# One exponential over two PSUM banks in the head of a fused attention and mixer kernel

## The chip, the cores and the metric

The kernel runs on one core of a Trainium2 chip. The metric is the device time of one execution in microseconds, the median of several; lower is better. The core's engines work side by side, each through its own queue in order: TensorE (PE), VectorE (DVE), ScalarE (ACT), GpSimd (POOL) and SyncE (SP), the last used for DMA alone. PSUM, where the matmuls write, is used as eight banks of 128 x 512 fp32 values.

## The reference

Two layers in a row, on 8 batches. The first is attention by random features (8 heads, 576 positions, 64 channels, 128 features), the second a mixer over tokens and channels.

```python
def phi(x):                                        # 128 features
    h = einsum('bhsd,md->bhsm', x, omega) - sum(x * x) / 2
    return exp(h - max(h)) / sqrt(m)
q_p, k_p = phi(q * scale), phi(k * scale)
kv  = einsum('bhsm,bhsd->bhmd', k_p, v);  z = sum(k_p, axis=2)
num = einsum('bhsm,bhmd->bhsd', q_p, kv)
den = einsum('bhsm,bhm->bhs', q_p, z)[..., None] + 1e-06
x = (num / den).transpose(0, 2, 1, 3).reshape(8, 576, 512)
h = maximum(x.transpose(0, 2, 1) @ w_tok1, 0) @ w_tok2     # 576 -> 256 -> 576
u = x + h.transpose(0, 2, 1)
out = u + maximum(u @ w_ch1, 0) @ w_ch2                    # 512 -> 1536 -> 512
```

## The kernel before, in words

All work is cut into some 1,200 jobs, each for one engine: a group of matmuls, an exponential, a copy, a DMA. `ORDER` is a list, written out in full, of the order in which the jobs are issued; a negative number there is a warming matmul on that bank, which computes nothing. `SLOT` gives, in the order in which they are asked for, the number of the buffer or PSUM bank that each job's result takes, and `MOVED` the jobs that run on another engine than usual. No scheduler decides anything later; each engine runs its jobs in the listed order, and semaphores keep the data in order between them. The eight banks are eight PSUM tiles, `bank0` to `bank7`.

A batch's 576 positions are 512 main positions and a tail of 64. For each batch the jobs are these:

- k and q come in. Batch 0's k is transposed on PE in fp32 (L470) and copied to `kT` (L286); q of batch 0 and k and q of batch 1 are transposed row by row in fp16 (`row_transposes`, L487) and copied to `qT` and `kT`. For k of batch 1, each of these copies has a small second one of the tails to `ktt` (four of 128 x 64). From batch 2 on, a DMA delivers them transposed.
- `attention`: for each of the four pairs of heads `hp`, `kp` (L642) and `qp` (L654) write the projected features of a pair into two banks, one for each half of the rows. Two exponentials for each, `kp_exp` and `qp_exp` (L516, 128 x 512, one for each bank), write `kp` and `qp` to SBUF. `km` (L666, L668) takes maxima of `kp` and their reciprocals on DVE; `vs` (L295) multiplies v by them, on POOL or DVE; `kv` (L687, with the tails L696) sums the products of `kp` and `vs`, and `kv_out` copies the result to `kvsb`. `num` (L720, L722) multiplies it with `qp` for one head, and `num_out` (L729, L730) divides on DVE; for two heads of batch 0 the division is a reciprocal on DVE (L739) and five scalings on ACT (L742).
- the tails: `kt` (L548), for batch 0 `kt_max` (L554) on DVE and four exponentials with that bias (L560); `qt` (L615) and `qt_exp`, two exponentials of 128 x 512 that read 256 columns each and write every value twice, to `qpt`.
- `token_mix_first` for batch 0: for each of four column blocks `db`, `t1` (L802, L803), a relu, `ut_` (L814, L816: x and the token product, summed in PSUM) and `ut_out`, the copy to `uT`. Later batches use `token_mix` and a transposing DMA.
- `channel_mix`: for each of 12 blocks `cb`, `c1` (L952) multiplies `uT` with a block of `wc1`, a relu follows, and `c2` (L986, for later batches L902) multiplies with `wc2`. For batch 0 and `cb` 0 and 1 the first product is split: `c1a` (L958) needs the first three blocks of `uT`, `c1b` (L960) the last.

The early part of the order mixes the attention of batches 0 and 1 with the loads of the weights; from the first `c1a` on, the products of one batch run beside the attention of the next.

Of the kernel before, what the change touches and what calls it, by code (L numbers as in the profile page):

```python
# [9 lines left out]
FP32 = mybir.dt.float32  # L10
# [71 lines left out]
]  # L82
SLOT = (
    "0001230450670021132045367010302617513012470262300513371400512200115470016321571004365170133427114615"
    "2706023150120733240065120734316732200715627122056371124763701250041207605411110007222613057312036204"
    "1375021106076210361724051016236170411507140350200761210416512307114506412733522052064330171260032070"
# [82 lines left out]
def kernel(  # L169
# [12 lines left out]
    nc = tc.nc  # L182
# [6 lines left out]
    P = 128  # L189
# [106 lines left out]

    def bank(name):
        return banks[place("bank", name)]

    def bank16(name):  # L300
        return bank(name).bitcast(FP16)

# [754 lines left out]
```

## Time and profile before

| | before |
|---|---|
| median of 3 runs | 278.24 us (277.53 to 278.56) |
| the profiled execution | 278.63 us, its span 276.8 us |
| PE busy | 269.2 us, 97% of the span, 2509 matmuls |
| DVE busy | 219.2 us, 79% |
| ACT busy | 141.1 us, 51% |
| POOL busy | 90.2 us, 33% |
| granted PE clock | 0.999 |

The span runs from the first to the last instruction that the profiler has; 1.83 us of the execution lie outside it. In the rows of the profile, names of buffers stand without their numbers, so that all of `bank0` to `bank7` are "bank". A row of a timeline gives the start and the duration in microseconds, the engine, the line, the operation with output and input, how many instructions the row holds, and in brackets the idle time of the engine before it with what ended it. A row of the chain of waits gives start, duration, engine, output and line of a piece of the chain that ended last.

### The profile page before, as it was taken

To read this page: it belongs to the slowest core of one execution; us is meant where nothing else is said; L and a number is where in the kernel's file an instruction comes from. 1 tells how busy PE (TensorE), PEld (TensorE's weight loads), DVE (VectorE), ACT (ScalarE), POOL (GpSimd) and SP (SyncE) were. 2 spreads that over 40 slices of the span, in tenths; PEclk is the share of its full clock that TensorE was granted. 3 is DMA by queue.
4 is the path that set the end of the run, shared out by engine and by line. 5 is a ranking of instruction groups with operands and counts; after the bars stand their busy time and mean duration, and the time that the engine had idled before them with its cause. 6 is when DMAs were issued, how large, how long until landed. Compare 5 with 4: busy or idle time off the path is not lost.

```text
span 276.8 us, 6243 instructions
## 1 busy us (share of the span) xinstructions
PE 269.2 (97%) x2509; PEld 167.5 (61%) x2509; DVE 219.2 (79%) x458; ACT 141.1 (51%) x296; POOL 90.2 (33%) x114
## 2 busy tenths in 40 slices
PE   7999999999999999999999999999999999999993
PEld 4467446455567655765676657755676477456782
DVE  2996948489996999996999899968985992685892
ACT  3999973288595237835756446635754500031200
POOL 8985482045812480076019510600043000000001
PEclk9999999999999999999999999999999999999999
DMA  7999999999999999869999994750252304030125
GB/s 194 193 204 204 198 201 183 203 160 147 206 207 142 221 182 163 206 120 167 176 202 175 252 109 129 170 113 2 85 90 77 96 0 94 2 152 0 78 82 147
DMA packets 81292, 39.66 MB, mean 143 GB/s; under 512 B 63984, under 2 KB 77040, under 8 KB 81072
## 3 DMA queue, kind: packets, MB, share of 16 engines
q0 software_dynamic: 31744, 17.74, 44.0%
q1 hardware_dynamic: 47360, 16.03, 28.3%
q10 hardware_dynamic: 2160, 5.51, 5.1%
q8 instruction: 19, 0.31, 0.4%
q14 instruction: 9, 0.07, 0.1%
HBM read 35.95 MB, written 16.52 MB: 189 GB/s over the span
## 4 chain that ended last, share of the span: by engine, by line
PE 87%; ACT 7%; DVE 3%; DMA 1%; issue 1%; ACTq 0%
PE bank L952 32%; PE bank L902 27%; PE bank L763 5%; PE bank L776 5%; PE bank L642 3%; PE bank L654 3%; PE bank L986 2%; PE bank L687 2%; PE bank L720 2%; ACT qp L516 2%; DMA wc<-in_k_dram 1%; DVE x L730 1%; PE bank L470 1%; ACT kp L516 1%; PE bank L830 1%; ACT r L290 1%
## 5 line engine op out<-in xcount | busy, mean ns | idle before, releaser
L290 ACT ACTIVATE r<-bank 128x512 f16<-128x512 f32 (+1 forms) x89 | 48.9, 599 | 82.5 <-PE bank L952 67.8
L952 PE MATMUL bank<-uT,wc 128*128 128x512 f16 x376 | 89.9, 379 | 0.0
L295 POOL TENSOR_TENSOR vs<-v,vs 128x512 f16<-128x512 f16 x31 | 32.7, 1060 | 91.8 <-DVE vs L668 62.5
L952 PEld LDWEIGHTS <-wc 128*128 128x128 f16 x424 | 38.6, 98 | 36.7 <-issue 0.3
L902 PEld LDWEIGHTS <-r 128*128 128x128 f16 x384 | 36.8, 98 | 8.8 <-issue 1.4
L516 ACT ACTIVATE qp<-bank 128x512 f16<-128x512 f32 x64 | 36.7, 633 | 9.3 <-PE bank L654 6.4
L516 ACT ACTIVATE kp<-bank 128x512 f16<-128x512 f32 x64 | 35.8, 626 | 7.3 <-PE bank L642 6.2
L666 DVE TENSOR_REDUCE km<-kp 128x8 f16<-128x1024 f16 x32 | 38.6, 1206 | 0.9 <-ACT kp L516 0.8
L730 DVE TENSOR_TENSOR x<-bank,rc 128x320 f16<-128x320 f32 x62 | 30.5, 491 | 2.1
L292 DVE TENSOR_SCALAR r<-bank 128x512 f16<-128x512 f32 (+1 forms) x37 | 24.6, 677 | 8.4 <-PE bank L952 7.5
L902 PEld LDWEIGHTS <-S 128*128 128x128 f16 x288 | 28.0, 98 | 5.1 <-issue 0.3
L902 PE MATMUL bank<-T,r 128*128 128x256 f16 x192 | 23.8, 273 | 0.0
L902 PE MATMUL bank<-wc,r 128*128 128x256 f16 x192 | 23.6, 273 | 0.0
L902 PE MATMUL bank<-T,S 128*128 128x256 f16 x192 | 23.4, 273 | 0.0
L891 DVE TENSOR_TENSOR o<-u,bank 128x512 f32<-128x512 f16 x28 | 19.0, 678 | 5.5 <-PE bank L902 5.4
L779 DVE TENSOR_TENSOR u<-x,bank 128x512 f16<-128x512 f16 x28 | 17.7, 680 | 4.9 <-PE bank L776 4.9
L931 POOL DMA_DIRECT2D out_dram<-o x2 | 1.3, 644 | 60.4 <-DVE o L891 60.4
L891 DVE TENSOR_TENSOR o<-o,bank 128x512 f32<-128x512 f32 (+1 forms) x27 | 16.5, 615 | 3.1 <-PE bank L902 2.6
L720 PEld LDWEIGHTS <-qp 128*128 128x128 f16 x256 | 13.7, 98 | 7.4 <-issue 0.3
L720 PE MATMUL bank<-kvsb,qp 128*128 128x65 f16 x256 | 15.4, 193 | 0.3 <-ACT kvsb L286 0.3
L729 DVE RECIPROCAL rc<-bank 128x5 f32<-128x5 f32 x62 | 11.4, 184 | 5.4 <-PE bank L722 4.2
L687 PEld LDWEIGHTS <-kp 128*128 128x128 f16 x256 | 11.2, 98 | 5.5 <-issue 0.9
(120 smaller groups left out, 381.6 us busy)
## 6 DMA issues: line engine op xcount, KB each, us to landing
out_dram<-o ACTq DMA_DIRECT2D x9, 512.0 KB, 2.7
q<-in_q_dram POOLq DMA_DIRECT2D x6, 576.0 KB, 9.9
wc<-in_moe_w_ch_dram POOLq DMA_DIRECT2D x4, 768.0 KB, 13.5
k<-in_k_dram POOLq DMA_DIRECT2D x6, 512.0 KB, 7.1
v<-in_v_dram POOLq DMA_DIRECT2D x6, 512.0 KB, 9.4
out_dram<-o SPq DMA_DIRECT2D x5, 512.0 KB, 3.8
r<-in_q_dram POOLq DMA_DIRECT2D x4, 288.0 KB, 5.4
v<-in_v_dram POOLq DMA_DIRECT2D x4, 256.0 KB, 10.1
```

The lines of the kernel that those rows point to most:

```text
L290: nc.scalar.activation(out=out, in_=in_, func=AF.Relu)
L292: nc.vector.tensor_relu(out=out, in_=in_)
L295: (nc.gpsimd if eng == "POOL" else nc.vector).tensor_tensor(**kw)
L516: nc.scalar.activation(out=out, in_=in_, func=AF.Exp, bias=0.0, scale=1.0)
L666: nc.vector.reduce_max(out=mx, in_=kpv, axis=AX.X)
L687: nc.tensor.matmul(ps[:, i, :], kpv[:, 2 * i + j // 2, j % 2, :], vs[:, i * NJ + j, 0 : D + 1], start=(i == 0 and j == 0), stop=False, ski ...
L720: nc.tensor.matmul(ps[:, k, j * 65 : (j + 1) * 65], st, s[:, i, 0 : D + 1], start=True, stop=True)
L730: nc.vector.tensor_tensor(out=t_x[place("x", b)][:, :, (2 * hp + hs[0]) * D : (2 * hp + hs[0] + n) * D].rearrange("p j (i d) -> p i j d", ...
L779: nc.vector.tensor_tensor(out=t_u[place("u", b)][:, j, :], in0=t_x[place("x", b)][:, j, :], in1=bank(n), op=ALU.add)
L891: nc.vector.tensor_tensor(out=o, in0=a, in1=ps, op=ALU.add)
L902: nc.tensor.matmul(ps[:, j * DH : (j + 1) * DH], a[:, cb, j * P : (j + 1) * P], w[:, cb, :], start=(bank_of(b, j0) not in held and j == j0 ...
L952: nc.tensor.matmul(ps, wc1[:, db, cb * P : (cb + 1) * P], moving(db), start=(db == 0), stop=(db == ND - 1))
```

## The change

The banks become slices of one PSUM tile, `all_banks`, so that one instruction can read two of them through a strided view (`pair_of`). For batches 0 and 1 the two exponentials of a pair of banks become one of 128 x 1024 (`kp_exp_both`, `qp_exp_both`): 32 exponentials become 16. The two banks are sorted by number first, so that the two halves may lie in either order. For batch 0, `qt_exp_once` writes the q tails once (512 columns) and `qt_dup` copies them on POOL. For batch 1, the four small copies of the k tails become one of 128 x 256, `k_tails`, which `MOVED` places on DVE. `ORDER`, `SLOT` and `MOVED` are new: the order of all engines, loads included, is another up to about the first channel product of batch 0, with small swaps behind it; 25 of the remaining jobs change between ACT and DVE, and there are 14 warming matmuls where there were 23.

```diff
-    banks = [pspool.tile([P, 512], FP32, name=f"bank{i}") for i in range(COUNT["bank"])]
+    all_banks = pspool.tile([P, COUNT["bank"], 512], FP32, name="bank")
+    banks = [all_banks[:, i, :] for i in range(COUNT["bank"])]
...
+    def both(n, any_order=True):
+        i = [place("bank", (n, e)) for e in range(2)]
+        return sorted(i) if any_order else i
+
+    def pair_of(n):
+        i, j = both(n)
+        return all_banks[:, i : j + 1 : j - i, :]
...
-                if w == "k":
-                    copy(eng, t_ktt[place("ktt", b)][:, h * RT : (h + 2) * RT].rearrange("p (h r) -> p h r", h=2), to[:, :, R:RA])
...
+        if b == 1:
+            e_ktt = engine("POOL")
+            def k_tails():
+                (nc.gpsimd if e_ktt == "POOL" else nc.vector).tensor_copy(out=t_ktt[place("ktt", b)].rearrange("p (h r) -> p h r", h=H), in_=rows_of(b, "k")[:, :, R:RA])
...
+        if b == 0:
+            def qt_exp_once():
+                o = t_qpt[place("qpt", b)][:, :, 0, :].rearrange("p h (r e) -> p e h r", e=2)
+                exp(o, pair_of(n_qt)[:, :, 0:256].rearrange("p e (h r) -> p e h r", h=H))
...
+            def qt_dup():
+                o = t_qpt[place("qpt", b)]
+                (nc.gpsimd if e_dup == "POOL" else nc.vector).tensor_copy(out=o[:, :, 1, :], in_=o[:, :, 0, :])
...
-            for e in range(2):
+            if not dma_in:
+                def kp_exp_both(n_k=n_k, hp=hp):
+                    exp(t_kp[place("kp", (b, hp))].rearrange("p c e m -> p e c m"), pair_of(n_k).rearrange("p e (c m) -> p e c m", c=4))
...
+            for e in range(2) if dma_in else ():
                 def kp_exp(e=e, n_k=n_k, hp=hp):
                     exp(t_kp[place("kp", (b, hp))][:, :, e, :], bank((n_k, e)).rearrange("p (c m) -> p c m", c=4))
...
+            if not dma_in:
+                def qp_exp_both(n_q=n_q, hp=hp):
+                    exp(t_qp[place("qp", (b, hp))], pair_of(n_q))
```

`dma_in` is true from batch 2 on. The new numbers of `ORDER`, `SLOT` and `MOVED` are left out here.

More of the change, by code (lines that the diff above doesn't have):

```diff
@@ L22 @@
 ORDER = [
[59 rows of a table removed]
[58 rows of a table added]
 ]
 SLOT = (
-    "0001230450670021132045367010302617513012470262300513371400512200115470016321571004365170133427114615"
-    "2706023150120733240065120734316732200715627122056371124763701250041207605411110007222613057312036204"
-    "1375021106076210361724051016236170411507140350200761210416512307114506412733522052064330171260032070"
-    "2511304120634017216372617462021504300762151043321530642151020025026324300102330114120061120041712506"
-    "2712607062170400122761152104033716002041516732322040041312300617100341061200131150227600413526401574"
@@ L89 @@
-    "3156007321243056114327206213024021607301230410313211123170420517632407350741520165207014225360701012"
-    "2420731402016310720013323411360113012420103046751416240153247100630105247110103520105165715621043510"
-    "76204060705032114"
+    "0001203450607012123604050017124305031126702041233617120350714250214170114506072043110514621021751465"
+    "1731023105046321701253107236235042011704021563401725234067511220024051700123345100607523141120207506"
+    "1102733452005130105060334250271610017546020751341162007204611523102673141325362511730622111270604017"
@@ L92 @@
+    "2233041517635411761321703517024256000312065043271620543160170226175024200112020114370051071041372605"
+    "2371503057134020173351406017132315010171615302022711010010207503101151021700411360723200541672504135"
+    "6412006374235012103576202243075321216314700501031713423110625042136252602564732417205263127011631142"
+    "2523604532611000321643020501010340612526001054371504256071523000410067523016111750267246326452001307"
+    "64150740573110206"
 )
 MOVED = {
-    42: "DVE", 46: "ACT", 48: "ACT", 52: "ACT", 56: "ACT", 58: "ACT", 59: "ACT", 61: "ACT", 62: "ACT", 65:
@@ L95 @@
-    "ACT", 86: "ACT", 128: "DVE", 138: "DVE", 142: "DVE", 144: "DVE", 150: "ACT", 156: "DVE", 160: "DVE", 162:
-    "DVE", 164: "ACT", 172: "ACT", 176: "DVE", 180: "ACT", 214: "ACT", 286: "DVE", 324: "ACT", 378: "DVE", 399:
-    "DVE", 426: "DVE", 428: "DVE", 432: "DVE", 434: "DVE", 484: "DVE", 498: "DVE", 552: "DVE", 556: "DVE", 562:
-    "DVE", 593: "ACT", 594: "ACT", 634: "DVE", 662: "DVE", 690: "DVE", 692: "DVE", 700: "DVE", 702: "DVE", 727:
-    "ACT", 768: "DVE", 796: "DVE", 822: "DVE", 828: "DVE", 830: "DVE", 836: "DVE", 838: "DVE", 863: "ACT", 904:
@@ L100 @@
-    "DVE", 970: "DVE", 997: "ACT", 998: "ACT", 1024: "DVE", 1052: "DVE", 1088: "DVE", 1092: "DVE", 1094: "DVE",
-    1096: "DVE", 1098: "DVE", 1102: "DVE", 1104: "DVE", 1108: "DVE", 1133: "ACT", 1134: "ACT", 1140: "DVE",
-    1148: "DVE", 1150: "DVE", 1152: "DVE", 1160: "DVE", 1200: "SP", 1205: "ACT", 1206: "SP", 1207: "ACT", 1208:
-    "SP",
+    44: "ACT", 46: "ACT", 50: "DVE", 52: "ACT", 53: "ACT", 58: "ACT", 61: "ACT", 64: "ACT", 65: "ACT", 67:
+    "ACT", 109: "ACT", 120: "DVE", 128: "DVE", 130: "DVE", 134: "DVE", 136: "DVE", 140: "DVE", 150: "DVE", 152:
@@ new lines @@
+    "DVE", 154: "DVE", 156: "ACT", 160: "DVE", 164: "ACT", 166: "DVE", 182: "ACT", 189: "DVE", 217: "ACT", 250:
+    "DVE", 271: "DVE", 309: "ACT", 363: "DVE", 384: "DVE", 411: "DVE", 413: "DVE", 417: "DVE", 419: "DVE", 469:
+    "DVE", 483: "DVE", 537: "DVE", 541: "DVE", 547: "DVE", 578: "ACT", 579: "ACT", 619: "DVE", 647: "DVE", 675:
+    "DVE", 677: "DVE", 685: "DVE", 687: "DVE", 712: "ACT", 753: "DVE", 781: "DVE", 807: "DVE", 813: "DVE", 815:
+    "DVE", 821: "DVE", 823: "DVE", 848: "ACT", 889: "DVE", 955: "DVE", 982: "ACT", 983: "ACT", 1009: "DVE",
@@ L104 @@
+    1037: "DVE", 1073: "DVE", 1077: "DVE", 1079: "DVE", 1081: "DVE", 1083: "DVE", 1087: "DVE", 1089: "DVE",
+    1093: "DVE", 1118: "ACT", 1119: "ACT", 1125: "DVE", 1133: "DVE", 1135: "DVE", 1137: "DVE", 1145: "DVE",
+    1185: "SP", 1190: "ACT", 1191: "SP", 1192: "ACT", 1193: "SP",
 }
@@ L494, in rows_out @@
                 copy(eng, to.rearrange("p h (c i) -> p h c i", i=RW // 2), bank16(names[o])[:, 0 : 2 * RA].rearrange("p (i h c) -> p h c i", i=RW // 2, h=2))
-                if w == "k":
-                    copy(eng, t_ktt[place("ktt", b)][:, h * RT : (h + 2) * RT].rearrange("p (h r) -> p h r", h=2), to[:, :, R:RA])
-            e = add(eng, 0.38 if w == "q" else 0.48, key if key_out is None else key_out, rows_out, deps=[t], take=[("ktt", b)] if w == "k" else [], give=[("bank", names[o])])
+            e = add(eng, 0.38, key if key_out is None else key_out, rows_out, deps=[t], give=[("bank", names[o])])
             for h in range(2):
@@ L543, in attention @@
         j_ktt = [tr["kt", b]] if b == 0 else src_of("k")
+        if b == 1:
+            e_ktt = engine("POOL")
+            def k_tails():
+                (nc.gpsimd if e_ktt == "POOL" else nc.vector).tensor_copy(out=t_ktt[place("ktt", b)].rearrange("p (h r) -> p h r", h=H), in_=rows_of(b, "k")[:, :, R:RA])
+            j_ktt = [add(e_ktt, 0.45, kkt, k_tails, deps=j_ktt, take=[("ktt", b)], give=[("kT", b)])]
         def kt():
@@ L612, in qt @@
         def qt():
-            ps, t = two(n_qt), rows_of(b, "q")
+            ps, t = [banks[i] for i in both(n_qt, b == 0)], rows_of(b, "q")
             for e in range(2):
@@ L617, in attention @@
         j_qte = []
-        for e in range(2):
+        if b == 0:
+            def qt_exp_once():
+                o = t_qpt[place("qpt", b)][:, :, 0, :].rearrange("p h (r e) -> p e h r", e=2)
+                exp(o, pair_of(n_qt)[:, :, 0:256].rearrange("p e (h r) -> p e h r", h=H))
+            j_qt1 = add("ACT", 0.5, kqe, qt_exp_once, deps=[j_qt], take=[("qpt", b)], give=two_of(n_qt))
+            e_dup = engine("POOL")
+            def qt_dup():
+                o = t_qpt[place("qpt", b)]
+                (nc.gpsimd if e_dup == "POOL" else nc.vector).tensor_copy(out=o[:, :, 1, :], in_=o[:, :, 0, :])
+            j_qte = [add(e_dup, 0.6, kqe, qt_dup, deps=[j_qt1])]
+        for e in range(2) if b else ():
             def qt_exp(e=e):
@@ L635, in kp @@
             def kp(n_k=n_k, hh=hh):
-                ps = [bank((n_k, e)) for e in range(2)]
+                ps = [banks[i] for i in both(n_k, not dma_in)]
                 for i in range(2):
@@ L645, in attention @@
             je = []
-            for e in range(2):
+            if not dma_in:
+                def kp_exp_both(n_k=n_k, hp=hp):
+                    exp(t_kp[place("kp", (b, hp))].rearrange("p c e m -> p e c m"), pair_of(n_k).rearrange("p e (c m) -> p e c m", c=4))
+                je.append(add("ACT", 0.9, at_["ke"], kp_exp_both, deps=[j_k], take=[("kp", (b, hp))], give=two_of(n_k)))
+            for e in range(2) if dma_in else ():
                 def kp_exp(e=e, n_k=n_k, hp=hp):
@@ L651, in qp @@
             def qp(n_q=n_q, hp=hp):
-                ps, t = [bank((n_q, e)) for e in range(2)], rows_of(b, "q")
+                ps, t = [banks[i] for i in both(n_q, not dma_in)], rows_of(b, "q")
                 for e in range(2):
@@ L657, in attention @@
             jq = []
-            for e in range(2):
+            if not dma_in:
+                def qp_exp_both(n_q=n_q, hp=hp):
+                    exp(t_qp[place("qp", (b, hp))], pair_of(n_q))
+                jq.append(add("ACT", 0.9, at_["qe"], qp_exp_both, deps=[j_q], take=[("qp", (b, hp))], give=two_of(n_q)))
+            for e in range(2) if dma_in else ():
                 def qp_exp(e=e, n_q=n_q, hp=hp):
```

117 rows, old and new, of the table ORDER are left out of this document.

## The prediction, on record before the run

> **What bounds the kernel now.** I read first the windows of ten microseconds, then the chain of waits up to 60 us, then the timelines of ScalarE (ACT), VectorE (DVE) and TensorE (PE) around the places that the chain names. The windows, with the busy time of each engine in each stretch:
>
> ```profile
> core 0 of [0], span 276.8 us
> 10.00:20.00 10.00, 9.08 (x147) 5.17 (x144) 9.46 (x19) 9.97 (x24) 9.17 (x12) 1.00 1.23 204
> 20.00:30.00 10.00, 9.54 (x162) 7.21 (x159) 7.51 (x20) 9.89 (x29) 4.77 (x6) 1.00 1.17 203
> 30.00:40.00 10.00, 10.00 (x59) 4.34 (x58) 7.02 (x13) 7.69 (x16) 7.28 (x8) 1.00 1.37 188
> ```
>
> After each stretch's length the columns are PE, PE's weight loads, DVE, ACT and POOL. From 10 to 30 us ACT is full (9.97 and 9.89 of 10), and DVE nearly so in the first of the two stretches (9.46). From 30 us on PE is full (10.00). So the kernel has a head that ACT and DVE set and a body that PE sets. The chain shows the seam:
>
> ```profile
> 12.96 1.47 ACT qp L516 x3
> 14.44 0.53 ACT qT L286
> 14.97 1.02 ACT kpt L560 x4
> 15.98 1.23 ACT qpt L516 x2
> 17.34 1.48 ACT qp L516 x3
> ...
> 22.72 2.06 ACT x L742 x10
> ...
> 30.30 1.29 PE bank L958 x6
> ...
> 33.54 5.29 PE bank L952 x24
> ```
>
> Piece after piece belongs to ACT until the first channel product of batch 0 (L958, the job c1a) starts on PE. Since PE has no room behind that point, c1a's start is what the head is worth: each microsecond by which it comes later or earlier is a microsecond of the end, unless PE finds idle time later. The change rewrites the head, and puts only small swaps behind it.
>
> **What the new instructions cost on ACT.** These rows of ACT's timeline give the slope:
>
> ```profile
> 7.63 1.09 ACT L516 ACTIVATE kp<-bank 128x512 f16<-128x512 f32 x2 [0.48 <-PE bank L642]
> ...
> 21.66 0.24 ACT L286 COPY ktt<-kT 128x64 f16<-128x64 f16 x1
> ...
> 24.59 0.74 ACT L290 ACTIVATE r<-bank 128x256 f16<-128x256 f32 x2
> 25.12 0.74 ACT L286 COPY qT<-bank 128x576 f16<-128x576 f16 x1
> ```
>
> Two operations of 256 columns take 25.12 - 24.59 = 0.53 us from start to start, 0.265 each; one of 512 takes 1.47 / 3 = 0.49 (chain). That is 0.88 ns a column and some 0.04 us that an instruction costs by itself. One exponential of 1024 columns should so take 0.49 + 512 x 0.88 ns = 0.94 us; with the shorter intervals elsewhere in the chain (0.48) it is 0.91. I take 0.92, against 0.98 for the two that it replaces: 16 of them save 16 x 0.06 = 1.0 us of ACT, about 0.7 of it ahead of c1a (12 of 16). The end of an instruction lies about 0.2 behind the start of the next (0.74 against 0.53), so another engine gets the result of a merged one some 1.05 to 1.1 us after its start, and both its banks only then; before, it got the first bank after half of that.
>
> On ScalarE the Trainium skill ("ScalarE: Activation LUTs", What ACT_TABLE_LOAD costs) has 186 ns and 0.833 ns a column, with 93 ns of overlap between neighbours. By that page a merged pair would save 0.09 us and all 16 of them 1.5; the slope agrees with the 0.88 of the rows, the fixed part is twice theirs.
>
> The q tails of batch 0: two exponentials, 1.23 us in the chain, become one of 512 columns (0.5) and a POOL copy off ACT's path: 0.7 saved. The k tails of batch 1: three of the four small copies sat on ACT at 0.24, 0.7 saved; the one large copy goes to DVE, for about what the fourth cost there. Together 0.7 + 0.7 + 0.7 = 2.1 us less on ACT ahead of c1a. The nine dropped warming matmuls are fill and worth nothing while PE waits for ACT in that stretch. The 25 jobs that change between ACT and DVE give back part: DVE gets two of the early relus and a k copy, and at 9.46 of 10 it is next in line. Half of 2.1, 1.1 us, is what I would expect from the work alone.
>
> **What the change adds without saying so: waits.** In the changed kernel all eight PSUM banks are one tile, and a merged exponential reads its two banks through one strided view. The waits of the changed program as built are taken over the whole stretch from the first bank to the last. The pairs that the new SLOT table hands out are mostly not neighbours (0 and 7, 0 and 5, 1 and 4, 2 and 7, 3 and 7, ...), so an exponential waits for, and is waited for by, users of banks that lie between and that it does not touch. There are 27 such waits up to the channel product of batch 0 and just behind it: 10 on PE, 11 on ACT, 6 on DVE. The program before has none of them. I walk the head with them. Each engine takes its instructions in order, so what stands behind a wait stands too.
>
> PE's and DVE's prices come from these rows:
>
> ```profile
> 11.04 0.60 PE L654 MATMUL bank<-qT,omT 64*128 64x512 f16 x4
> ...
> 13.02 2.00 PE L1024 MATMUL bank<-S 128*128 128x512 f16 x8 [0.22 <-ACT kp L516]
> ...
> 16.57 0.52 PE L487 MATMUL bank<-ident,r 64*128 64x64 f16 x18
> 17.39 0.28 PE L720 MATMUL bank<-kvsb,qp 128*128 128x65 f16 x4 [0.30 <-ACT kvsb L286]
> ```
>
> ```profile
> 12.87 0.76 DVE L554 TENSOR_REDUCE kt_nb<-bank 128x2 f32<-128x256 f32 x2
> ...
> 16.53 1.16 DVE L295 TENSOR_TENSOR vs<-v,vs 128x512 f16<-128x512 f16 x1
> 17.96 0.19 DVE L729 RECIPROCAL rc<-bank 128x5 f32<-128x5 f32 x1 [0.26 <-PE bank L722]
> 18.18 0.49 DVE L730 TENSOR_TENSOR x<-bank,rc 128x320 f16<-128x320 f32 x1
> 18.59 0.18 DVE L729 RECIPROCAL rc<-bank 128x5 f32<-128x5 f32 x1
> ...
> 23.43 0.68 DVE L286 CAST uT<-bank 128x512 f16<-128x512 f32 x1
> ```
>
> *Up to 15.4 us.* The first exponential now needs both banks of its pair, so it starts near 8.05 rather than 7.63, and ACT is free at 9.0. The second (banks 0 and 7) waits for the maxima of the k tails, which DVE takes from bank 6 (0.76 us, put forward in the new order). With the tail copy and PE's tail products ahead of them I put their end at 9.95, an estimate. So ACT idles 1.0 us, and runs two merged exponentials to 11.8. The transposes of k heads 2 and 3 into bank 4 may start only when the one over banks 0 to 7 is done, 11.05; with 0.6 for them, 0.53 each for the three copies behind, and 1.02 for the four tail exponentials, the last k exponential starts at 14.45 and frees ACT at 15.35.
>
> *15.4 to 22 us.* From here ACT and PE go in turns. A warming matmul in bank 3 waits for the exponential over 2 and 4 (15.55), then 0.25 for it and 0.3 for the q product: the next exponential starts at 16.2. It covers 1 to 3, and the kv product in bank 2 waits for it (17.25); ACT does the q tails (0.5) and the kv copy, and starts the next at 18.05. That one covers 0 to 5; the row transposes of batch 1's k (bank 3, 0.52) wait until 19.1; the next exponential, over 1 to 4, waits for these, 19.55; the q product of the last pair (bank 2) waits for that one, 20.6; the last q exponential runs from 20.95 to 21.85. In PE's queue the kv product that DVE's next copy wants stands behind the held row transposes, so that DVE stands idle from about 17.5 to 20.05. With that copy and the 1.16 us of vs, its first L729 comes at 21.4 instead of 17.96, 3.4 us late.
>
> *22 us to c1a.* DVE then has six pairs of L729 and L730 (18.59 - 17.96 = 0.63 each, 3.8), two reciprocals alone (0.4), a kv copy (0.3), a kT copy (0.75) and two relus (0.8), and half a microsecond of waits: 21.4 + 6.5 = 27.9 for the first copy of uT, which is at 23.43 now, 4.5 late. Now comes a lock step. One uT product takes about 0.9, by these rows (29.26 to the next product at 30.14):
>
> ```profile
> 29.26 0.61 PE L814 MATMUL bank<-ident,x 128*128 128x128 f16 x4
> ...
> 29.67 0.64 PE L816 MATMUL bank<-w,r 128*128 128x512 f16 x2
> ...
> 30.14 1.46 PE L958 MATMUL bank<-uT,wc 128*128 128x512 f16 x6
> ```
>
> The exponential over banks 2 to 7 waits for the uT product in bank 5 (28.7) and is done at 29.8; the uT copy out of bank 5 waits for it, 30.5; the one over 4 to 6 waits for that copy, done at 31.6; q's row transposes in bank 5 wait for this, 32.0, and a uT product behind them goes to 32.95; the one over 0 to 2 waits for that, done at 34.05; the uT copy out of bank 1 waits for it, 34.8. c1a needs that copy: 34.85 instead of 30.14, **4.7 us late**. I give DMA no part in it: everything here comes later than now, so that a transfer has more time.
>
> *Behind c1a.* Two channel products stand behind such exponentials too: the second c1a in bank 5 behind the one over 3 to 7 (0.8 us) and a later one in bank 3 behind the one over 2 to 5 (1.0 us). They lie in PE's full stretch, so up to 1.8 us more; at the other end nothing, if the exponentials get ahead while PE works. The walk is roughest here, since it rests on all the steps ahead of it; I take 0.6, nearer to nothing, as PE's queue gives each of these exponentials at least one channel product of time.
>
> **The sum.** On the profiled execution (278.63 us, 1.83 of it outside the span): +4.7 + 0.6 = 5.3, 283.9. That execution is 0.39 above the median of the runs, 278.24, so the forecast is 283.5. The saved ACT time is inside it, since the walk uses the new prices.
>
> **The rivals.**
> (a) *The waits are met before they are asked for, and the work counts.* It decides at the first of them: if the maxima of the tails end before 9.05, and the row transposes before the exponential ahead has ended, ACT keeps running as it does now. Then the work alone stays: 1.1 us with DVE next in line, 277.1; 2.1 us if DVE keeps pace, 276.1. For it speaks ACT's full row now; against it that eight of these waits run in a ring between ACT and PE, where each side's wait starts only when the other has ended. The Trainium skill ("PSUM — Partial Sum Buffer", PSUM bank collisions raise a hardware error) has each bank as a memory of its own, to be guarded by bank and quadrant. By that rule the 27 waits guard nothing, and a program built by it would go to these two times. But this one holds the waits, and no run here shows it without.
> (b) *They cost just what the work saves.* If only the first idle of ACT (1.0) counts, it meets the 1.1 gained: 278.1.
> (c) *More is lost than I walk.* All 1.8 us behind c1a, and PE with fewer warming matmuls at a lower clock (the windows show 1.00 now): at half the clock PE's links in the ring, some 1.5 us, double. 278.24 + 4.7 + 1.8 + 1.5 = 286.2.
>
> **How the numbers follow.** About 0.5% (1.4 us) is what a measurement of this kernel can tell from no change. The forecast and (c) together 0.77 (0.65 and 0.12), all slower by more than that. (a) has 0.19: 0.10 at 276.1, faster, and 0.09 at 277.1, inside 0.5%. (b) 0.04, also inside. So faster 0.10, same 0.13, slower 0.77. The forecast's own range: a third of the lock step could be hidden, 4.7 - 1.8 = 2.9, which gives 281.1, up to (c)'s 286.2. The whole range goes down to (b): 278.0 to 286.5, which leaves out most of (a), and a little above.
>
> **What would show it.** In the new profile the first c1a (now L989) starts near 34.9; ACT shows gaps of 0.5 to 1 us ahead of its exponentials between 9 and 21 us and again from 28 to 36, released by DVE's maxima, PE's row transposes and uT copies, things in other banks than those it reads; DVE idles near 17.5 to 20; merged exponentials start 0.9 us apart where they stand in a row. The ACT busy share of 10:30 falls clearly below 9.9. The prediction is wrong if ACT's row stays full there, or if c1a starts before 31; its size is wrong if PE makes up time behind c1a, with idle rows in the body that are not in the present trace.

## The result, and the profile after

The changed kernel takes 290.56 us (289.55 to 290.76), the one before 278.19 beside it: 1.0441 times as long, 95% interval 1.0422 to 1.0461. The profiled execution took 290.63 us against 278.63, its span 288.9 against 276.8. Slower was forecast, and the cause named; but 283.5 us was forecast, and the measured time lies 4 us above the upper end of the range. Single executions of some kernels below took 284 to 289 us where the others of the same kernel took 277 to 282 (two of ten in the second experiment, three of twelve in the ninth, one each in the tenth and twelfth); the factors with their intervals leave these out, the medians hold them.

The windows of the changed kernel, with the same columns as before:

```profile
core 0 of [0], span 288.9 us
10.00:15.00 5.00, 3.24 (x55) 1.74 (x56) 4.30 (x8) 4.44 (x10) 4.61 (x5) 1.00 1.29 206
15.00:20.00 5.00, 2.24 (x29) 0.91 (x30) 3.05 (x5) 3.96 (x6) 1.61 (x4) 1.00 0.99 179
20.00:25.00 5.00, 4.55 (x79) 3.03 (x74) 2.70 (x8) 3.18 (x7) 4.98 (x7) 0.55 0.99 152
25.00:30.00 5.00, 5.00 (x89) 4.53 (x88) 3.68 (x12) 2.76 (x9) 3.51 (x5) 0.77 1.31 192
30.00:40.00 10.00, 7.19 (x93) 4.85 (x91) 6.86 (x14) 7.22 (x12) 1.28 (x3) 1.00 1.24 205
40.00:60.00 20.00, 18.39 (x156) 9.12 (x155) 13.48 (x31) 8.70 (x16) 9.10 (x11) 1.00 1.02 144
60.00:100.00 40.00, 39.42 (x355) 21.97 (x354) 33.16 (x61) 26.60 (x55) 15.06 (x18) 1.00 0.94 153
```

ACT, full from 10 to 30 us before, is at 8.4 of 10 and then at 5.9; no other engine has taken its place. From 15 to 20 us PE works 2.24 of 5 us, and right behind that its clock is granted at 0.55 and 0.77: from 20 to 30 us PE looks busy because much of its work runs at half speed (the eight matmuls of a kv product take 0.63 us at 23.3 us, 0.42 at 17.9). ACT's timeline shows what the exponentials wait for:

```profile
10.56 1.94 ACT L522 ACTIVATE kp<-bank 128x1024 f16<-128x1024 f32 x2 [1.02 <-DVE kt_nb L565]
...
16.80 1.02 ACT L522 ACTIVATE qp<-bank 128x1024 f16<-128x1024 f32 x1 [0.79 <-PE bank L679]
...
20.31 1.02 ACT L522 ACTIVATE qp<-bank 128x1024 f16<-128x1024 f32 x1 [0.51 <-PE bank L495]
22.00 1.02 ACT L522 ACTIVATE qp<-bank 128x1024 f16<-128x1024 f32 x1 [0.67 <-PE bank L679]
...
33.27 1.02 ACT L522 ACTIVATE kp<-bank 128x1024 f16<-128x1024 f32 x1 [0.54 <-DVE uT L286]
```

The first, the third and the last wait for something in a bank that they do not read: the maxima of the k tails, batch 1's row transposes, a copy of uT. And the waits of PE, up to the first channel product and behind it:

```profile
PE bank L478 <- ACT kp L522: 1.9, 1, 1.9
PE bank L495 <- ACT kp L522: 1.2, 1, 1.2
PE bank L1053 <- ACT kp L522: 1.2, 1, 1.2
PE bank L495 <- ACT qp L522: 1.1, 1, 1.1
```

```profile
PE bank L749 <- ACT qp L522: 1.0, 1, 1.0
PE bank L987 <- ACT qp L522: 0.7, 1, 0.7
PE bank L981 <- ACT qp L522: 0.6, 1, 0.6
```

Every one is PE waiting for an exponential. In the kernel before, no wait of PE in this stretch adds up to more than 0.3 us; its longest up to the first channel product is

```profile
PE bank L720 <- ACT kvsb L286: 0.3, 1, 0.3
```

The signs that the prediction named are there: ACT's gaps and what ends them, DVE idle for 2.8 us up to 20.99, ACT's row no longer full. The first channel product is L987 here (the prediction called it L989, which is the second part, c1b).

### The profile page after: what moved, and what is told of

Its sections match the earlier page's. It is cut to its first block, busy times and chain, and to the rows that moved or that the text cites. A ratio compares the mean times of both kernels' runs of the same rounds, so it can differ in the third digit from the quotient of the medians.

```text
span 288.9 us, 6207 instructions
## 1 busy us (share of the span) xinstructions
PE 271.6 (94%) x2501; PEld 169.2 (59%) x2501; DVE 223.5 (77%) x463; ACT 138.3 (48%) x271; POOL 91.5 (32%) x115
## 4 chain that ended last, share of the span: by engine, by line
PE 80%; DVE 7%; ACT 6%; DMA 3%; issue 1%; DVEq 0%; ACTq 0%
PE bank L981 27%; PE bank L931 25%; PE bank L805 4%; PE bank L792 4%; PE bank L716 3%; PE bank L749 3%; PE bank L679 2%; PE bank L663 2%; ACT qp L522 2%; PE bank L1015 2%; ACT kp L522 2%; DVE T L456 2%; DMA out_dram<-o 2%; DMA wc<-in_k_dram 1%; PE bank L478 1%
## 5 line engine op out<-in xcount | busy, mean ns | idle before, releaser
L290 ACT ACTIVATE r<-bank 128x512 f16<-128x512 f32 (+1 forms) x85 | 46.8, 604 | 81.3 <-PE bank L981 68.3
L295 POOL TENSOR_TENSOR vs<-v,vs 128x512 f16<-128x512 f16 x31 | 33.4, 1083 | 91.4 <-DVE vs L697 62.3
L522 ACT ACTIVATE qp<-bank 128x512 f16<-128x512 f32 (+1 forms) x56 | 35.6, 675 | 10.3 <-PE bank L679 6.1
L522 ACT ACTIVATE kp<-bank 128x512 f16<-128x512 f32 (+1 forms) x56 | 34.9, 678 | 10.3 <-PE bank L663 7.7
L292 DVE TENSOR_SCALAR r<-bank 128x512 f16<-128x512 f32 (+1 forms) x41 | 26.8, 665 | 15.1 <-PE bank L981 11.6
L931 PE MATMUL bank<-T,S 128*128 128x256 f16 x192 | 23.3, 273 | 0.3 <-DVE o L920 0.3
```

Source lines behind the costliest of these rows:

```text
L290: nc.scalar.activation(out=out, in_=in_, func=AF.Relu)
L292: nc.vector.tensor_relu(out=out, in_=in_)
L295: (nc.gpsimd if eng == "POOL" else nc.vector).tensor_tensor(**kw)
L522: nc.scalar.activation(out=out, in_=in_, func=AF.Exp, bias=0.0, scale=1.0)
L931: nc.tensor.matmul(ps[:, j * DH : (j + 1) * DH], a[:, cb, j * P : (j + 1) * P], w[:, cb, :], start=(bank_of(b, j0) not in held and j == j0 ...
```

## The experiments

The theory (A): the waits over the banks in between cost the time. The rivals: the new order itself is worse (B), or the dropped warming matmuls let PE's clock fall and that costs the time (C). There are 22 of these matmuls in the kernel before and 14 in the changed one, by `ORDER` and by the traces, so eight were dropped; the 23 and the nine in the texts written ahead of the runs are one too many.

**One: no merged exponentials, the new order kept.**

```diff
-    all_banks = pspool.tile([P, COUNT["bank"], 512], FP32, name="bank")
-    banks = [all_banks[:, i, :] for i in range(COUNT["bank"])]
+    banks = [pspool.tile([P, 512], FP32, name=f"bank{i}") for i in range(COUNT["bank"])]
...
-                    exp(t_qp[place("qp", (b, hp))], pair_of(n_q))
+                    for e in range(2):
+                        exp(t_qp[place("qp", (b, hp))][:, e, :], banks[both(n_q)[e]])
```

> The changed kernel with its order, banks and engines kept, but the eight banks as eight tiles again and each merged exponential (and the one of the q tails) split into two, one for each bank. So the waits across banks are gone, the new order stays. Theory A (the waits over the banks in between cost the time, the lost PE clock being one of their consequences): 276 to 280 us, granted clock 1.00 from 20 to 30 us, first channel product (L987 in the changed kernel) near 29 to 31 us. Theory B (the new order itself is worse): 285 us or more, with the first channel product near 37 still. Theory C (fewer warming matmuls let PE's clock fall, which costs the time): the clock is 0.66 from 20 to 30 us again, and the time 286 to 290.

Measured: 278.75 us, 1.0038 times the kernel before (1.0006 to 1.007). The windows and the first channel product of this kernel:

```profile
15.00:20.00 5.00, 4.12 (x91) 2.95 (x89) 4.59 (x10) 4.87 (x15) 4.04 (x6) 1.00 1.14 208
20.00:25.00 5.00, 5.00 (x94) 4.23 (x92) 4.65 (x14) 4.25 (x14) 4.59 (x6) 1.00 1.16 204
```

```profile
29.15 0.82 PE L986 MATMUL bank<-uT,wc 128*128 128x512 f16 x3
```

The order is not to blame: with the same 14 warming matmuls the clock stays at 1.00 in this stretch of the profiled execution, and the first channel product is 1.0 us ahead of the kernel before (the first exponential comes at 7.62 and 7.63 us in the two, so this is not a matter of the start). B and C fall as causes of the 12 us.

**Two: merged, with other bank numbers.** Only `SLOT` (and the banks of the warming matmuls) is written anew, so that the two banks of each pair are neighbours and nothing lies between them. 296 of its 717 numbers change, all of them numbers of banks.

```diff
 SLOT = (
-    "0001203450607012123604050017124305031126702041233617120350714250214170114506072043110514621021751465"
+    "0501200430706512120703045016123354001127603021230617134350271254311120171546023017104501221431650215"
...
```

> The changed kernel with only the bank numbers changed, so that both banks of every merged exponential are neighbours; order, engines and merged exponentials stay as they are. Waits across banks: one is left of 28. Theory A: 276 to 279 us, and no slower than the split kernel by more than 0.5 us, since the merged exponentials save about 1 us of ACT. Theory B: 285 or more. A rival on the merging itself (both banks come free only at the end of the long exponential): 2 us or more above the split kernel.

Measured: 278.52 us, 1.0026 times (1.0002 to 1.005). This is the changed kernel with its order, its engines and its merged exponentials; only the numbers of the banks differ, and 12.0 us are gone. The profiled execution, 280.6 us, was one of the longer ones; its clock fell for a while too, as shown at the end. Merging does save what was forecast where exponentials stand in a row:

```profile
7.39 2.86 ACT L457 ACTIVATE kp<-bank 128x1024 f16<-128x1024 f32 x3
10.11 0.62 ACT L221 CAST kT<-bank 128x512 f16<-128x512 f32 x1
```

(10.11 - 7.39) / 3 = 0.91 us each, where 0.92 was forecast and two single ones take 0.98.

**Three: the waits kept, the clock kept up.** 16 warming matmuls more in the four gaps of PE. The edit in words:

```text
ORDER: 5 x bank 1 ahead of the first q products, 3 x bank 4 ahead of the first kv product,
       5 x bank 7 ahead of the row transposes of batch 1's k, 3 x bank 5 ahead of the last q product
```

> The changed kernel with 16 warming matmuls more, put into the four stretches between 14.9 and 21.5 us in which PE stood idle, on banks that no exponential in flight covers. Theory A: the clock stays at 1.00, but the waits stay, so only what PE's work at half clock cost comes back: 1.5 to 3 us, 287.5 to 289. Theory C: most of the 12 us come back, below 283. Theory B: 287 to 291.

Measured: 287.89 us, 1.0337 times (1.0313 to 1.0361).

```profile
15.00:20.00 5.00, 5.00 (x58) 2.26 (x58) 2.22 (x5) 3.97 (x5) 2.91 (x5) 1.00 1.10 196
20.00:25.00 5.00, 4.27 (x98) 3.62 (x97) 4.17 (x12) 3.94 (x10) 5.00 (x8) 1.00 1.09 174
```

```profile
34.42 0.81 PE L929 MATMUL bank<-uT,wc 128*128 128x512 f16 x3 [0.31 <-DVE uT L228]
```

In the profiled execution (286.70 us) the clock is at 1.00, and the first channel product is at 34.4. By the medians 2.7 of the 12.4 us are gone (290.56 - 287.89). Some of the clock was still lost in the other three executions, whose mean is 0.990 to 0.994, so 2.7 is rather too little for it. The rest, most of the 12.4 us, is there with the clock kept up too.

**Four: only the merging, on the old order.** The kernel before with one tile and merged exponentials, at the place of the first of each two; bank numbers, order and all 22 warming matmuls as they were.

> The kernel before with its order, engines and bank numbers, but the banks as one tile and the two exponentials of each pair of batches 0 and 1 merged at the place of the first of them. Nothing else of the change. Theory A: the waits across banks appear here too (29 of them), on an order that was not made for them: 282 to 292 us. Theory B: 277 to 279, as the kernel before or a little faster. Theory C: 277 to 279, as all 23 warming matmuls are there.

Measured: 287.84 us, 1.0349 times (1.0313 to 1.0384). So one tile and a strided view are enough to lose 9.7 us; the new order is not needed for it. Nor is the clock: in the profiled execution (287.14 us) it is at 1.00 through the whole head, and 8.5 us are lost all the same.

**Six and seven: the two groups of waits by themselves.** `SLOT` changed for batch 0's pairs alone (19 numbers), and for batch 1's alone (22 numbers).

> The changed kernel with neighbouring banks for the merged exponentials of batch 0 alone (19 bank numbers changed): the 10 waits of batch 0 are gone, the 18 of batch 1 stay, and with them the lock step of the uT copies and the two channel products behind exponentials. If the two groups add up (stretch from the first uT copy to the first channel product 7.0 us in the changed kernel against 4.6 in the one with all neighbours, and from there to the k tails of batch 2 28.4 against 25.7): 278.5 + 2.4 + 2.7 = 283.6, between 282 and 285. If one group alone explains all: 278 to 280 or 289 to 291.

> The changed kernel with neighbouring banks for batch 1 alone (22 bank numbers changed): the 18 waits of batch 1 are gone, the 10 of batch 0 stay, with the turns that ACT and PE take from 10 to 22 us and PE's clock falling behind them. If the groups add up (the first uT copy is at 30.5 us in the changed kernel against 26.2 with all neighbours): 278.5 + 4.4 = 282.9, between 281.5 and 285, clock below 0.8 in 20:30. If one group alone explains all: 278 to 280 or 289 to 291.

Measured: 284.25 us (1.0237, 1.0193 to 1.028) with batch 1's waits left, 284.97 (1.0251, 1.0222 to 1.0281) with batch 0's left. Over the 278.52 of the kernel without either, that is 5.7 and 6.5 us, together 12.2, and both at once measured 12.0: they add up. Batch 0's group comes out 2.1 us dearer than expected, batch 1's 0.7. With batch 0's waits left the clock is 0.83 from 20 to 30 us, where less than 0.8 was expected, and 0.66 from 10 to 15.

**Eight: merging on the old order with neighbouring banks.**

> The kernel before with its own order, the exponentials of batches 0 and 1 merged, and bank numbers changed so that the two banks are neighbours; two waits across banks are left of 29. Theory A: the 9.7 us of the merged kernel with the old bank numbers are gone, 277 to 279 us. Of the merging itself: ACT saves about 0.7 us ahead of the first channel product, but an exponential now needs both banks filled and frees both late: 277.3 if the first counts, 279 if the second does.

Measured: 278.53 us, 1.0021 times (1.0007 to 1.0034). The 9.7 us are gone here too, and the merging by itself brings nothing: 0.2% slower, if anything.

**Eleven: the light parts alone**, on the kernel before: q tails written once and copied on POOL, k tails in one copy on DVE.

> The kernel before with two parts of the change alone, in its own order and banks: the q tails of batch 0 written once (two exponentials of 256 columns instead of two of 512) and copied on POOL, and the k tails of batch 1 in one copy on DVE instead of four small ones. They take 0.7 + 0.7 us off ACT ahead of the first channel product. If ACT alone sets the head: 276.8 to 277.3. If the POOL copy (behind the vs of POOL, which ends at 17.15 us) holds the first num products back, or DVE is next: 278 to 278.6.

Measured: 278.48 us, 1.0009 times (0.999 to 1.0028). In its profile the first copy of uT comes at 23.98 instead of 23.43 and the first channel product at 29.97 instead of 30.14: the 1.4 us taken off ACT do not reach the seam.

**Five and twelve: where the new order loses its lead.** The split kernel is 1.0 us ahead at its first channel product and at 55 us, and behind from 70 us on. DVE's rows and POOL's in it, and in the kernel before:

```profile
61.55 1.20 DVE L452 TENSOR_TENSOR T<-wc 128x1536 f16<-128x1536 f16 x1
62.79 1.70 DVE L452 TENSOR_TENSOR T<-wc,T 128x1536 f16<-128x1536 f16 x1
...
61.86 1.81 POOL L294 TENSOR_TENSOR vs<-v,vs 128x512 f16<-128x512 f16 x1
```

```profile
54.45 0.95 DVE L448 TENSOR_TENSOR T<-wc 128x1536 f16<-128x1536 f16 x1
64.14 0.94 DVE L448 TENSOR_TENSOR T<-wc,T 128x1536 f16<-128x1536 f16 x1
...
62.40 1.05 POOL L295 TENSOR_TENSOR vs<-v,vs 128x512 f16<-128x512 f16 x1 [1.24 <-DVE vs L668]
```

The new order has moved the first of these jobs by 7 us, out of a stretch in which DVE had time (it stood idle for 3.8 us up to 52.65) into one in which DVE works without a break. It has also set both beside a POOL operation: 0.95 and 0.94 become 1.20 and 1.70, and POOL's 1.05 becomes 1.81. The three end 2.94 us after the first has started (61.55 to 64.49), and alone they take 0.95 + 0.94 + 1.05 = 2.94: they took turns, and nothing was won by the overlap. The edits move one job number, then a second, in `ORDER`.

> The split kernel of the first experiment with one job moved: the first of the four differences of w_ch2 on DVE (T, 0.95 us) goes back from behind the last output copy of batch 0 (61.5 us) to its place in the kernel before, ahead of the last uadd of batch 1 (near 53). In the split kernel the first channel product is 1.0 us earlier than in the kernel before (29.15 against 30.14) and the k tails of batch 2 too (54.75 against 55.78), but from 70 us on it is 0.2 us late: 1.2 us are lost between, while DVE works without a break from 61 to 81 us. Theory D (DVE binds there because T was moved into it): the lead of 1.0 stays, 277.0 to 277.7 us, PE with less than 0.2 us of idle between 60 and 100. Rival (the transfers or PE's own swaps lose it): 278.4 to 279.

> The split kernel with both of the first two differences of w_ch2 on DVE put back where the kernel before has them: the first between the uadds of batch 1 (as in the fifth experiment), the second behind the last km but one of batch 2. In the split kernel the two stood at 61.55 and 62.79 us and took 1.20 and 1.70 us, beside a vs of POOL that took 1.81; in the kernel before they took 0.95 and 0.94, and POOL's vs 1.05. In the fifth experiment the second still ran beside POOL's vs and took 2.06. Theory D, sharpened (two-input operations of DVE and POOL that run at the same time slow each other, and DVE has no gap from 61 to 81 us to absorb it): both at 0.95 us, no lead lost between 55 and 100 us, 277.1 to 277.8 where the clock stays at 1.00 in the head. Rival (the lead is lost to something else, or the head's lead itself comes and goes): 278.2 to 278.8.

Measured: 278.28 us (1.0012, 0.9992 to 1.0032) with the first moved, 278.83 (1.0036, 1.0012 to 1.006) with both. With the first moved alone, the second still ran beside POOL, and here it alone was the longer for it:

```profile
62.92 2.06 DVE L394 TENSOR_TENSOR T<-wc,T 128x1536 f16<-128x1536 f16 x1
...
63.09 1.07 POOL L236 TENSOR_TENSOR vs<-v,vs 128x512 f16<-128x512 f16 x1
```

With both moved, DVE's two are as short as before; the second still lies beside a vs, and now POOL's is the longer one:

```profile
53.28 0.95 DVE L394 TENSOR_TENSOR T<-wc 128x1536 f16<-128x1536 f16 x1
62.76 0.94 DVE L394 TENSOR_TENSOR T<-wc,T 128x1536 f16<-128x1536 f16 x1
...
62.99 1.61 POOL L236 TENSOR_TENSOR vs<-v,vs 128x512 f16<-128x512 f16 x1 [0.43 <-PE bank L657]
```

In that profiled execution (277.57 us) the lead over the kernel before is 1.6 us at the k tails of batch 2 on PE (54.21 against 55.78) and 0.9 at those of batch 4 (115.20 against 116.12), where the split kernel goes from 1.0 ahead to 0.2 behind. So the place of T makes about half of the 1.2 us that the split kernel loses: with both jobs back, 0.65 are still lost (1.57 to 0.92), and where they go no run shows. And the median does not move, as the rival had it: the executions of this kernel spread from 277.45 to over 280 us, with clocks from 1.000 down to 0.985, while those of the kernel before stay within 277.4 and 278.5. The head's lead comes and goes. What may take it shows in the profile of the fifth experiment, where the first channel product comes at 30.09: PE waits there for the load of batch 1's k, and 1.5 us later its clock falls. In the kernel before, PE waits for no load between 7 and 31 us.

```profile
16.14 0.44 PE L433 MATMUL bank<-ident,r 64*128 64x64 f16 x18 [1.75 <-DMA r<-in_k_dram]
```

**Nine and ten: more warming matmuls for the kernels without the waits.** Eleven, ahead of the jobs at which PE stood idle.

> The split kernel with T moved back (the fifth experiment) and 11 warming matmuls more, placed on long-free banks ahead of the jobs at which PE stood idle between 9 and 19 us: 25 in all, where the kernel before has 23 and the changed one 14. In the fifth experiment's profile the clock was 0.88 from 10 to 20 us, and the first channel product came at 30.1; in the first experiment's it was 1.00 and the product at 29.15. Theory E (with too few warming matmuls the clock falls in some executions, and the lead of 1.0 us is lost there): clock 1.00 from 10 to 30 us, first channel product near 29.2, executions closer together than before (277.73 to 280.0), median 277.0 to 277.7. Rival (the loads of the inputs set the head in this order): 278 to 278.6.

> The same for the kernel with neighbouring banks and merged exponentials: T moved back, 11 warming matmuls more. In the second experiment the clock was 0.85 from 20 to 30 us in the profiled execution (280.6 us, first channel product at 30.8), and two executions were at 287 to 288. Theory E: clock 1.00, 276.8 to 277.6, and at most 0.5 us below the split one (what the merging saves on ACT), if DVE is not next in line; equal to it if it is. Rival on the merging (both banks come free late): 0.5 us or more above the split one.

Measured: 279.55 us (1.0048, 1.0031 to 1.0066) and 279.57 (1.0058, 1.0032 to 1.0084). The theory behind them fails: the clock did stay at 1.00 from 10 to 30 us in the profiled executions, and the kernels became slower. The chain of waits of the ninth points to the reason: the fill stands on it, ahead of the work for which ACT and DVE wait. In the first experiment, without this fill, the chain from 12 to 19 us is ACT's alone.

```profile
14.74 0.54 PE bank L994 x2
15.28 0.25 PE bank L657 x8
15.52 0.11 PE bank L666 x2
15.63 0.32 PE bank L619 x2
15.96 0.97 PE bank L994 x4
16.93 0.37 PE bank L433 x18
```

L994 is the fill there: 1.5 us of it in this stretch alone. No version beats the kernel before.

## Why the prediction was wrong, step by step

| step | forecast | measured in the changed kernel |
|---|---|---|
| ACT waits for the maxima, second exponential at | 10.0 us | 10.56 |
| first q exponential | 16.2 | 16.80 |
| last q exponential of batch 0 | 20.95 | 22.00 |
| first reciprocal of num_out on DVE | 21.4 | 22.46 |
| first copy of uT | 27.9 | 30.54 |
| from there to the first channel product | 6.95 | 7.04 |
| first channel product | 34.85 | 37.58 |

```profile
30.54 0.68 DVE L286 CAST uT<-bank 128x512 f16<-128x512 f32 x1
```

```profile
37.58 0.59 PE L987 MATMUL bank<-uT,wc 128*128 128x512 f16 x2 [0.31 <-DVE uT L286]
```

*Right:* what bounds the kernel, the waits and the turns up to the first channel product, the lock step to a tenth of a microsecond, and the price of a merged exponential. The waits are shown, not argued: bank numbers alone remove 12.0 us, and putting the waits onto the old order costs 9.7.

*Wrong: the size, 6.7 us short on the profiled execution (5.3 forecast, 290.63 - 278.63 = 12.0 measured).* Three terms of the sum were mis-sized.

1. *Up to the first channel product, 2.7 us, most of it the clock.* About 0.5 of it is the start: the first exponential came at 8.52 us in this execution, where the walk had 8.05. It came at 7.62, 7.39 and 7.17 in the profiles of the first three experiments, which share the order, so this part looks like chance. From the first exponential to the first channel product the changed kernel takes 29.1 us (37.58 - 8.52) and the third experiment, with the same waits and the clock kept up, 27.3 (34.42 - 7.17): about 1.8 is the clock, lost between 20 and 30 us. The walk has 26.8 for this (34.85 - 8.05), so 0.4 is left for its own steps. The walk ran PE at full clock; the halved one stood in rival (c), with 0.12 of chance and 1.5 us. It had the gaps of PE after which the clock fell, and the dropped warming matmuls beside them, and called those "worth nothing while PE waits for ACT".

2. *Behind the first channel product, 2.7 us instead of 0.6.* From there to the k tails of batch 2 the changed kernel takes 28.35 us, the kernel with neighbouring banks 25.66 and the one before 25.64. Three waits make 2.3 of it (the 1.0, 0.7 and 0.6 shown above). Two (0.7 and 0.6) had been priced together at 1.8 and then cut to 0.6 with the argument that PE's queue gives the exponentials time. It did not: they came to 1.3, and PE is full there otherwise, so each stall counts. The third, num in bank 2 behind the exponential over 1 to 7, was not on the list, and is the longest. The last 0.4 stays open.

3. *The rest of the body, about 1.9 us instead of nothing.* The prediction took the "small swaps" behind the head for nothing. Between the k tails of batch 2 and of batch 4, 1.2 us are lost, in the split kernel, in the one with neighbouring banks, and in the changed one alike (10.15 us behind the kernel before at the first, 11.34 at the second). By the twelfth experiment the place of the T jobs makes about half of that. The cause of the other half, and of the last 0.7 us behind it, stays open.

2.7 + 2.1 + 1.9 = 6.7.

Rival (a) did not come true as told, but the second experiment shows its condition, a program without these waits. It gives 278.5 where (a) had 276.1 to 277.1. The light parts alone give nothing either, nor does the merging alone (the eleventh and eighth experiment), so the 2.1 us of ACT were worth nothing, not 1.1. That other waits than ACT's were about as late would explain it, but no run here shows which. The Trainium skill ("PSUM — Partial Sum Buffer", PSUM bank collisions raise a hardware error) has each bank guarded by itself. The runs agree as far as they go: the program with no waits across banks (the first experiment) and the one with a single one left (the second) run 12 us faster than the changed kernel.

## What to carry to other kernels

When several buffers are joined into one tile so that an instruction can read two of them, ask what range the waits are taken over: a strided view may wait for everything between its ends, and choosing neighbouring buffers can be the whole difference. Read the waits of the program as built before believing in saved work. And when stalls are added to PE, price a lost clock with the stall, not as a chance beside it; but fill against it can itself get in the way. When single profiles are compared, look at where the work starts: the first exponential of one and the same order of the head came between 6.8 and 8.5 us.

## What the runs showed of the hardware

*The clock fell to one half without a long idle gap.* From 15 to 20 us PE worked 45% of the time in the changed kernel (2.24 of 5), its longest gap there being 1.2 us, and 1.9 the longest before it (up to 11.64). In finer windows the granted clock is exactly one half for a while, and the 0.55 and 0.77 are means over that and full clock:

```profile
20.25:20.50 0.25, 0.25 (x12) 0.25 (x10) 0.00 (x0) 0.19 (x1) 0.23 (x2) 0.95 1.80 97
20.50:20.75 0.25, 0.25 (x7) 0.11 (x3) 0.00 (x0) 0.25 (x1) 0.25 (x1) 0.50 0.98 37
...
27.00:27.25 0.25, 0.25 (x6) 0.25 (x4) 0.25 (x1) 0.25 (x2) 0.00 (x0) 0.50 1.43 199
27.25:27.50 0.25, 0.25 (x7) 0.25 (x5) 0.08 (x1) 0.25 (x1) 0.00 (x0) 0.90 1.46 199
```

It is at one half for 6.8 us here, and for 3.4 us in the second experiment (19.5 to 22.9) and in the fifth (17.7 to 21.1). The second fell after 64%:

```profile
15.00:20.00 5.00, 3.19 (x64) 2.13 (x64) 4.84 (x9) 3.51 (x7) 4.74 (x8) 0.95 1.13 206
20.00:25.00 5.00, 5.00 (x94) 4.48 (x95) 3.65 (x11) 2.96 (x10) 3.70 (x5) 0.71 1.16 207
```

But the busy share of such a window does not settle it: with 55% the fourth experiment stayed at 1.00,

```profile
10.00:15.00 5.00, 2.76 (x39) 1.19 (x33) 3.77 (x8) 4.61 (x6) 4.31 (x5) 1.00 1.28 204
15.00:20.00 5.00, 3.89 (x54) 2.04 (x52) 4.07 (x6) 3.76 (x10) 3.41 (x5) 1.00 1.17 193
```

and the first with 82% (4.12 of 5). A half-empty stretch can be enough, and need not be; no run here shows the rule.

The Trainium skill ("TensorE: Matmul & The Clock Gate", Part 1: The HAM clock gate) gives half the clock after an idle window of some 3.4 us, and tells in the same part of a kernel whose clock oscillated because PE was idle for short times, often. The half agrees with the 0.50. The changed kernel's trace is nearer to the second, since no gap of PE between 9 and 20 us was as long as 3.4.

*Two-input operations on DVE and POOL took turns where they met*, as the rows of T and vs show. The time that one of them waits falls on DVE (0.94 to 2.06, with POOL's at 1.07), on POOL (1.05 to 1.61, with DVE's at 0.94) or on both (0.94 to 1.70 and 1.05 to 1.81). The Trainium skill ("GPSIMD Engine Reference", 1. Specifications) names the shared SBUF interface, with contention for DVE instructions that have two SBUF inputs; these rows agree.
